# One pass over four row groups for the attention scores, with the values in the spare columns of the same banks

## The chip, the cores and the metric

The kernel runs on one core of one Trainium2 chip. The metric is the time of one execution on the device in microseconds (us), given as the median of several executions. Most executions of one kernel agree within 0.3%. For each one the mean granted clock of TensorE is known as well, as a share of full speed. One execution of each version was profiled. Below, a group of matmuls *holds the queue* from its first start to the first start of the group behind it.

## The reference

Windowed attention with eight batches, eight heads, 576 positions and 64 channels is followed by a feed-forward network (FFN) that multiplies two projections.

```python
scores = scale * np.matmul(q, k.transpose(0, 1, 3, 2))
rel = pos[:, None] - pos[None, :]
mask_plain = (rel >= 0) & (rel < 32)                         # heads 0 to 3
mask_dil = (rel >= 0) & (rel < 128) & (rel % 4 == 0)         # heads 4 to 7
attn = softmax(where(masks, scores, -1e9))                   # (shortened)
x = (attn @ v), heads side by side: 4608 tokens x 512
h = (x @ w1) * (x @ w2) @ w3                                 # 512 -> 1024 -> 1024
out = h @ w_out                                              # -> 4608 x 512, float32
```

The kernel multiplies `w3` and `w_out` into one matrix first. Below this is called fusing.

## The kernel before

The attention is cut into 32 steps: eight batches (called blocks here), two sets of four heads, two halves of the positions. Each step has four parts on TensorE: scores for heads 0 and 1, scores for heads 2 and 3, values (the product of exponentials and v), and transposes of the result. In between stand FFN matmuls of 128x512, so that the softmax on ScalarE and VectorE has time. `scores` of the kernel before, cut to what matters:

```python
ps_s = psum.tile([P, 2, TB], F32, name="ps_s")      # two banks for scores
ps_o = psum.tile([P, 2, TB], F32, name="ps_o")      # two banks for values
def scores(self, hp, sp):                           # hp: which pair of heads
    for m in range(3 * hf, 3 * hf + 3):
        for c in range(2):                          # two halves of the 64 channels
            for g in range(2):
                prt = slice(32 * (2 * hp + g), 32 * (2 * hp + g) + 32)
                nc.tensor.matmul(out=sp[:, g, c0 : c0 + 96], lhsT=kt[prt, ...], rhs=..., ...)
    nc.scalar.activation(out=ev, in_=sp[:, :, 0:HALF], func=ACT.Exp, scale=scale)  # 576 columns
    nc.vector.tensor_tensor(out=ev, in0=ev, in1=mk..., op=AL.mult)                 # mask
def values(self):                                   # twelve matmuls into ps_o, then
    nc.vector.reciprocal(out=rcp[0:96], in_=ov[:, :, :, D])
    nc.vector.tensor_tensor(out=xo[0:96], in0=ov[:, :, :, 0:D], in1=rcp..., op=AL.mult)
```

The parts are put into a list of phases, block by block. `segment(lo, hi)` pipelines the steps lo to hi-1. There are three segments: block 0, block 1, blocks 2 to 7. A function `point()` in the FFN code runs the next phases at given places. The transposes of q and k (on VectorE) were phases of their own.

The softmax here doesn't subtract the row's maximum and nothing guards it: scores larger than these inputs give would overflow.

## Time and profile before

The kernel before takes 289.62 us (median of 3 executions, 289.61 to 290.29).

| busy, us of a span of 288.0 | TensorE matmul | weight load | VectorE | ScalarE | GpSimd |
|---|---|---|---|---|---|
| before | 260.3 (90%) | 131.8 | 164.8 (57%) | 123.8 (43%) | 53.7 |

From 75 us on TensorE never stops, so its queue sets the end. What it doesn't show is the list of TensorE's waits. Each line gives what waited, what ended the wait, the sum in us, how often, and the longest:

```profile
PE ps_s L258 <- DVE kt L230: 10.1, 2, 9.1
PE ps_s L258 <- DVE kt L223: 2.7, 1, 2.7
PE ps_x L312 <- ACT w3T L461: 2.3, 2, 1.2
PE ps_x L312 <- DVE xo L297: 1.8, 2, 1.3
```

The first two are mostly the start, where the first q and k are loaded and transposed. The name to keep in mind is `xo`, the normalised result of a step: before, no scores (`ps_s`) ever waited for it.

### The profile page before, as it was taken

How to read it: one execution, taken by the hardware profiler on the slowest of the kernel's cores; microseconds unless marked ns; L12 is line 12 of the kernel's file. 1: busy time of each engine (PE TensorE's matmuls, PEld its weight loads, DVE VectorE, ACT ScalarE, POOL GpSimd, SP SyncE). 2: the span in 40 equal slices, each digit the busy share in tenths (PEclk: the TensorE clock that was granted, in tenths of full speed). 3: DMA queues.
4: the chain of work that ended last, by engine and by line, in shares of the span. 5: the costliest groups of instructions: out<-in, count | busy, mean ns of one | idle time of the engine just before them, and what ended most of it. 6: DMA issues, size and time to landing. Idle time of an engine off the chain costs nothing.

```text
span 288.0 us, 5662 instructions
## 1 busy us (share of the span) xinstructions
PE 260.3 (90%) x2336; PEld 131.8 (46%) x2336; DVE 164.8 (57%) x356; ACT 123.8 (43%) x200; POOL 53.7 (19%) x77
## 2 busy tenths in 40 slices
PE   0466988879899999999999999999999999999994
PEld 0353435444345545444444445445545544444441
DVE  5573385545798776767677767776764443222110
ACT  1543245543446455444544454455444433332422
POOL 8943512350042042006000600000000000000000
PEclk9999999999999999999999999999999999999999
DMA  7999999999069289567907991111111121111133
GB/s 102 156 207 190 198 211 210 202 194 144 0 102 171 75 166 173 80 116 130 137 36 124 145 147 42 39 36 39 39 36 39 36 56 55 36 73 36 48 85 126
DMA packets 50746, 30.51 MB, mean 106 GB/s; under 512 B 37920, under 2 KB 40992, under 8 KB 50720
## 3 DMA queue, kind: packets, MB, share of 16 engines
q0 software_dynamic: 45088, 20.71, 57.5%
q1 hardware_dynamic: 5632, 9.44, 10.9%
q8 instruction: 18, 0.29, 0.4%
q14 instruction: 8, 0.07, 0.1%
HBM read 41.41 MB, written 9.44 MB: 177 GB/s over the span
## 4 chain that ended last, share of the span: by engine, by line
PE 82%; DMA 9%; POOL 3%; ACT 2%; DVE 2%; issue 1%; POOLq 0%; ACTq 0%
PE f L406 41%; PE f L439 22%; PE ps_s L258 7%; DMA qn<-in_q_dram 5%; DMA w_sb<-in_moe_w_dram 4%; PE f L469 4%; PE ps_o L287 4%; PE ps_x L312 3%; PE ps_x L455 1%; ACT w3T L461 1%; POOL vst L137 1%; POOL vp L128 1%; POOL w_sb L155 1%; ACT et L268 0%; POOL qn L113 0%
## 5 line engine op out<-in xcount | busy, mean ns | idle before, releaser
L406 PE MATMUL f<-XT,w_sb 128*128 128x512 bf16 x576 | 138.8, 383 | 2.0 <-DMA w_sb<-in_moe_w_dram 1.3
L417 DVE TENSOR_TENSOR gt<-f,asb 128x512 bf16<-128x512 f32 x72 | 49.5, 687 | 55.5 <-PE f L406 55.3
L406 PEld LDWEIGHTS <-w_sb 128*128 128x128 bf16 x576 | 52.5, 98 | 61.1 <-issue 3.1
L439 PE MATMUL f<-wf_sb,gt 128*128 128x512 bf16 x288 | 70.8, 379 | 0.0
L416 ACT CAST asb<-f 128x512 bf16<-128x512 f32 x72 | 42.2, 586 | 54.3 <-PE f L406 49.6
L268 ACT ACTIVATE et<-ps_s 128x576 bf16<-128x576 f32 x60 | 39.2, 653 | 40.1 <-PE ps_s L258 39.9
L447 ACT COPY osb<-f 128x512 f32<-128x512 f32 x36 | 21.1, 586 | 45.7 <-PE f L439 45.7
L258 PE MATMUL ps_s<-qt,kt 32*128 32x96 bf16 x720 | 26.9, 206 | 13.8 <-DVE kt L230 10.1
L439 PEld LDWEIGHTS <-gt 128*128 128x128 bf16 x288 | 25.2, 98 | 25.2
L258 PEld LDWEIGHTS <-kt 32*128 32x128 bf16 x768 | 19.3, 97 | 37.0 <-issue 20.2
L297 DVE TENSOR_TENSOR xo<-ps_o,rcp 96x768 bf16<-96x768 f32 x32 | 30.5, 953 | 1.1
L137 POOL DMA_DIRECT2D vst<-in_v_dram x32 | 21.3, 672 | 13.9 <-DMA w3n<-in_moe_w_dram 4.4
L270 DVE TENSOR_TENSOR et<-et,mask_pl 128x576 bf16<-128x576 bf16 x32 | 14.6, 457 | 15.8 <-ACT et L268 15.5
L270 DVE TENSOR_TENSOR et<-et,mask_di 128x576 bf16<-128x576 bf16 x32 | 14.6, 456 | 14.7 <-ACT et L268 14.5
L230 DVE STREAM_TRANSPOSE qt<-qn 128x160 uint32<-128x160 uint32 (+1 forms) x64 | 19.6, 421 | 1.9 <-DMA qn<-in_q_dram 1.9
L287 PEld LDWEIGHTS <-et 128*128 128x128 bf16 x384 | 17.0, 102 | 7.7 <-issue 1.2
L312 PE MATMUL ps_x<-ident,xo 96*128 96x96 bf16 x192 | 14.4, 215 | 5.4 <-ACT w3T L461 2.3
L312 PEld LDWEIGHTS <-xo 96*128 96x128 bf16 x192 | 11.9, 102 | 12.5 <-DVE xo L297 4.1
L113 POOL DMA_DIRECT2D qn<-in_q_dram x9 | 6.3, 696 | 61.1 <-DVE qt L230 57.9
L296 DVE RECIPROCAL rcp<-ps_o 96x12 f32<-96x12 f32 x32 | 7.2, 225 | 16.4 <-PE ps_o L287 16.3
L469 PE MATMUL f<-wo_sb,w3T 128*128 128x512 bf16 x64 | 16.0, 380 | 0.0
L327 ACT COPY XT<-ps_x 128x576 bf16<-128x576 bf16 x18 | 11.5, 640 | 7.7 <-PE ps_x L312 7.7
(43 smaller groups left out, 113.8 us busy)
## 6 DMA issues: line engine op xcount, KB each, us to landing
qn<-in_q_dram POOLq DMA_DIRECT2D x7, 576.0 KB, 8.7
kn<-in_k_dram POOLq DMA_DIRECT2D x7, 576.0 KB, 7.8
vp<-in_v_dram POOLq DMA_DIRECT2D x7, 384.0 KB, 9.8
w_sb<-in_moe_w_dram POOLq DMA_DIRECT2D x4, 512.0 KB, 11.9
w3n<-in_moe_w_dram POOLq DMA_DIRECT2D x4, 512.0 KB, 18.7
out_dram<-osb SPq DMA_DIRECT2D x8, 256.0 KB, 2.3
out_dram<-osb SPq DMA_DIRECT2D x8, 224.0 KB, 2.3
out_dram<-osb SPq DMA_DIRECT2D x8, 192.0 KB, 2.2
```

The lines of the kernel that those rows point to most:

```text
L137: nc.gpsimd.dma_start(out=vsts[b % 2][p0 : p0 + n, m, :, :], in_=bass.AP(tensor=x.tensor, offset=x.offset + (4 * i0 + 2 * second) * D, ap= ...
L258: nc.tensor.matmul(out=sp[:, g, c0 : c0 + 96], lhsT=kt[prt, 96 * m : 96 * m + P, c], rhs=rhs, start=(c == 0), stop=(c == 1),)
L268: nc.scalar.activation(out=ev, in_=sp[:, :, 0:HALF], func=ACT.Exp, scale=scale)
L270: nc.vector.tensor_tensor(out=ev, in0=ev, in1=mk.unsqueeze(1).to_broadcast([P, 2, HALF]), op=AL.mult)
L287: nc.tensor.matmul(out=ps_o[:, hp, j * (D + 1) : (j + 1) * (D + 1)], lhsT=self.et[:, c0 : c0 + P], rhs=rhs, start=True, stop=True,)
L297: nc.vector.tensor_tensor(out=xo[0:96], in0=ov[:, :, :, 0:D], in1=rcp[0:96].unsqueeze(3).to_broadcast([96, 2, 6, D]), op=AL.mult,)
L312: nc.tensor.transpose(out=xo, in_=self.xo[0:96, hp, 2 * m : 2 * m + 2, :], identity=ident[0:96, 0:96],)
L406: nc.tensor.matmul(out=ps, lhsT=w_sb[:, c, f * P : (f + 1) * P], rhs=XT[:, c, t0 + lo : t0 + hi], start=(c == 0), stop=(c == DCH - 1),)
L416: nc.scalar.copy(out=a_sb[:, 0 : hi - lo], in_=ps)
L417: nc.vector.tensor_tensor(out=gts[t][:, f, lo:hi], in0=pss[1], in1=a_sb[:, 0 : hi - lo], op=AL.mult)
L439: nc.tensor.matmul(out=y, lhsT=gts[t][:, f, tb * P : (tb + 1) * P], rhs=wf_sb[:, f, :], start=(f == 0), stop=(f == KFF - 1),)
L469: nc.tensor.matmul(out=ps, lhsT=w3T[ft][:, g, :], rhs=wo_sb[:, g, :], start=(g == 0), stop=(g == KFF - 1),)
```

## The change

The intent is to compute the scores of all four heads in one pass. Head h lies on partitions 32h to 32h+31, which is called a row group here, so four heads fill four groups. The four results go to four banks (in this kernel slices of 512 float32 columns of the memory that takes TensorE's results). With the banks thus taken, the values go to the unused columns of the same banks (288 columns are scores, then 195 are values). The exponential and the mask become one instruction each, of 1152 columns. The core of the diff:

```diff
-    ps_s = psum.tile([P, 2, TB], F32, name="ps_s")
-    ps_o = psum.tile([P, 2, TB], F32, name="ps_o")
+    ps_a = psum.tile([P, 4, TB], F32, name="ps_a")
...
-        def scores(self, hp, sp):
+        def scores(self):
...
-                    for g in range(2):
-                        prt = slice(32 * (2 * hp + g), 32 * (2 * hp + g) + 32)
+                    for h in range(4):
+                        prt = slice(32 * h, 32 * h + 32)
...
+            n = 2 if self.b == 0 else 4
+            for h in range(0, 4, n):      # exponential and mask of n heads at once
...
+            if self.b == 0:
+                ov = ps_e[:, :, 0 : ns * (D + 1)]
+            else:
+                ov = ps_a[:, :, HALF : HALF + ns * (D + 1)]
...
-                later(lambda st=st: st.scores(0, s_tile(0)))
+                later(st.scores)
...
-                later(lambda st=st: st.scores(1, s_tile(1)))
                 if at == 0:
-                    later(transpose_qk, b, 0, 0)
+                    if i == lo:
+                        behind(transpose_qk, b, 0, 0)
...
```

`later` makes a phase of its own and `behind` hangs a function to the phase before it. Thus there are fewer phases, and they fall at other places between the FFN matmuls. From block 1 on the change also moves the transposes of q and k to earlier places; at the start of a segment two of them now fall behind the same scores.

More of the change, by code (lines that the diff above doesn't have):

```diff
@@ L258, in scores @@
                         nc.tensor.matmul(
-                            out=sp[:, g, c0 : c0 + 96],
+                            out=ps_a[:, h, c0 : c0 + 96],
                             lhsT=kt[prt, 96 * m : 96 * m + P, c],
@@ L264, in scores @@
                         )
-            ev = self.et[:, 2 * hp * HALF : 2 * (hp + 1) * HALF].rearrange(
-                "p (g x) -> p g x", g=2
-            )
-            nc.scalar.activation(out=ev, in_=sp[:, :, 0:HALF], func=ACT.Exp, scale=scale)
             mk = (mask_di if u else mask_pl[:, hf]).rearrange("p m x -> p (m x)")
-            nc.vector.tensor_tensor(
-                out=ev, in0=ev, in1=mk.unsqueeze(1).to_broadcast([P, 2, HALF]), op=AL.mult
-            )
+            n = 2 if self.b == 0 else 4
+            for h in range(0, 4, n):
+                ev = self.et[:, h * HALF : (h + n) * HALF].rearrange("p (g x) -> p g x", g=n)
+                nc.scalar.activation(
+                    out=ev, in_=ps_a[:, h : h + n, 0:HALF], func=ACT.Exp, scale=scale
+                )
+                nc.vector.tensor_tensor(
+                    out=ev, in0=ev, in1=mk.unsqueeze(1).to_broadcast([P, n, HALF]), op=AL.mult
+                )
         def values(self):
@@ L277, in values @@
             self.xo = xo = wk_pool.tile([P, 2, 6, D], BF16, tag="xo", bufs=3, name="xo")
+            nb = 2 if self.b == 0 else 4
+            ns = 12 // nb
+            if self.b == 0:
+                ov = ps_e[:, :, 0 : ns * (D + 1)]
+            else:
+                ov = ps_a[:, :, HALF : HALF + ns * (D + 1)]
+            ov = ov.rearrange("p n (j e) -> p n j e", e=D + 1)
             for hp in range(2):
@@ L280, in values @@
                     for hl in range(2):
-                        h, j = 2 * hp + hl, 2 * m + hl
+                        h, j = 2 * hp + hl, 6 * hp + 2 * m + hl
                         if self.u == 0:
@@ L287, in values @@
                         nc.tensor.matmul(
-                            out=ps_o[:, hp, j * (D + 1) : (j + 1) * (D + 1)],
+                            out=ov[:, j // ns, j % ns, :],
                             lhsT=self.et[:, c0 : c0 + P],
@@ L293, in values @@
                         )
-            rcp = wk_pool.tile([P, 2, 6], F32, tag="rcp", name="rcp")
-            ov = ps_o[0:96, :, 0 : 6 * (D + 1)].rearrange("p h (j e) -> p h j e", e=D + 1)
-            nc.vector.reciprocal(out=rcp[0:96], in_=ov[:, :, :, D])
+            rcp = wk_pool.tile([P, nb, ns], F32, tag=f"rcp{nb}", name="rcp")
+            nc.vector.reciprocal(out=rcp[0:96], in_=ov[0:96, :, :, D])
             nc.vector.tensor_tensor(
-                out=xo[0:96],
-                in0=ov[:, :, :, 0:D],
-                in1=rcp[0:96].unsqueeze(3).to_broadcast([96, 2, 6, D]),
+                out=xo[0:96].rearrange("p h j d -> p (h j) d").rearrange(
+                    "p (n s) d -> p n s d", n=nb
+                ),
+                in0=ov[0:96, :, :, 0:D],
+                in1=rcp[0:96].unsqueeze(3).to_broadcast([96, nb, ns, D]),
                 op=AL.mult,
@@ L327, in to_channels @@
                 nc.scalar.copy(out=dst, in_=xv)
-    early = [True]
     steps = [
@@ L346, in prefetch, with behind, run @@
             load_vp(b)
-    def s_tile(hp):
-        return ps_e if early[0] and hp else ps_s
     def later(f, *args):
-        phases.append(lambda: f(*args))
+        phases.append([lambda: f(*args)])
+    def behind(f, *args):
+        phases[-1].append(lambda: f(*args))
+    def run(phase):
+        for f in phase:
+            f()
     def segment(lo, hi):
@@ L366, in segment @@
                     later(spread_vd, b)
-            if at == 2 and more:
-                later(transpose_qk, b + 1, 1, 0)
-            if at == 3 and more:
-                later(transpose_qk, b + 1, 1, 1)
             if st is not None:
-                later(lambda st=st: st.scores(0, s_tile(0)))
+                later(st.scores)
             if p2 is not None:
@@ L378, in segment @@
             if st is not None:
-                later(lambda st=st: st.scores(1, s_tile(1)))
                 if at == 0:
-                    later(transpose_qk, b, 0, 0)
+                    if i == lo:
+                        behind(transpose_qk, b, 0, 0)
                     if b == 0:
-                        later(spread_vd, 0)
+                        behind(spread_vd, 0)
+                    else:
+                        behind(transpose_qk, b, 0, 1)
                 if at == 1:
-                    later(transpose_qk, b, 0, 1)
-                    later(prefetch, b + 2)
+                    if b == 0:
+                        behind(transpose_qk, b, 0, 1)
+                    behind(prefetch, b + 2)
+                    if more:
+                        behind(transpose_qk, b + 1, 1, 0)
+                if at == 2 and more:
+                    behind(transpose_qk, b + 1, 1, 1)
+                    behind(spread_vd, b + 1)
                 if at == 3 and more:
-                    later(spread_vd, b + 1)
+                    behind(transpose_qk, b + 1, 0, 0)
     segment(0, 4)
@@ L493 @@
     for ph in phases[:n0]:
-        ph()
-    early[0] = False
+        run(ph)
     stage.close()
@@ L511, in point @@
         while state[1] < want:
-            phases[state[1]]()
+            run(phases[state[1]])
             state[1] += 1
```

## The prediction

> **What bounds the kernel now.** I read the page's busy table and slices first, then the busy time by stage, then the order of instructions of one steady stretch in the timeline, then the waits that end TensorE's idle time.
>
> ```profile
> 37.30:75.10 37.80, 32.47 (x332) 17.75 (x332) 22.15 (x48) 16.53 (x22) 9.58 (x12) 1.00 1.25 176
> 75.10:102.70 27.60, 27.54 (x317) 14.21 (x318) 22.37 (x52) 14.26 (x24) 6.17 (x8) 1.00 0.75 101
> 102.70:230.50 127.80, 127.80 (x1234) 64.04 (x1233) 87.15 (x179) 61.85 (x104) 15.73 (x20) 1.00 0.54 86
> ```
>
> These are stages: first the stretch, its length, then busy us of TensorE matmul, weight load, VectorE, ScalarE, GpSimd. Before 37.3 us TensorE waits for data: two FFN weight halves land at 37.31 and end a wait of 1.32 us. From 37.3 to 75.1 block 1's attention runs beside the fusing of two weight matrices, with 5.3 us of TensorE idle. From 75 us to the end TensorE does not stop: every nanosecond of its queue is on the path that sets the end. ScalarE (61.85 of 127.80) and VectorE (87.15) have room. So what counts is the time the TensorE queue needs, and any new wait in it.
>
> The same queue at one steady place, by the starts of its groups:
>
> ```profile
> 153.88 0.62 PEld L287 LDWEIGHTS <-et 128*128 128x128 bf16 x12
> 154.09 0.53 PE L287 MATMUL ps_o<-vd,et 128*128 128x65 bf16 x12
> 154.37 0.69 DVE L417 TENSOR_TENSOR gt<-f,asb 128x512 bf16<-128x512 f32 x1 [0.80 <-PE f L406]
> ...
> 154.46 1.02 PE L439 MATMUL f<-wf_sb,gt 128*128 128x512 bf16 x4
> 154.97 0.22 DVE L296 RECIPROCAL rcp<-ps_o 96x12 f32<-96x12 f32 x1
> 155.23 0.95 DVE L297 TENSOR_TENSOR xo<-ps_o,rcp 96x768 bf16<-96x768 f32 x1
> 155.42 0.29 PEld L258 LDWEIGHTS <-kt 32*128 32x128 bf16 x12 [0.42 <-issue]
> 155.42 0.43 PE L258 MATMUL ps_s<-qt,kt 32*128 32x96 bf16 x12
> ...
> 155.78 0.55 PEld L439 LDWEIGHTS <-gt 128*128 128x128 bf16 x4
> 155.78 1.04 PE L439 MATMUL f<-wf_sb,gt 128*128 128x512 bf16 x4
> ```
>
> Four FFN matmuls take 0.86 us (0.216 each; eight elsewhere 1.73). Twelve value matmuls hold the queue 0.37 (154.09 to 154.46). But 154.46 to 155.42 is 0.96, so 0.10 is lost on entering the 32-row scores; the twelve score matmuls then hold it 0.36 to 155.78, and the first full matmul after them is some 0.01 late. One half of the scores (two heads) thus costs 0.47 us, two halves per step 0.94. A six-fold transpose group costs 0.26 (152.11 to 152.37). Sum per step: 0.94 + 0.37 + 0.26 = 1.57; with 24 FFN matmuls (5.18) that is 6.75, and the pattern does repeat after 26.99 us for four steps.
>
> Inside the 0.36 there are six rounds of two concurrent matmuls. The records last about 0.20, twelve span 0.43, so the last starts 0.23 after the first: some 43 ns per round, however many row groups are in it.
>
> **What the Trainium skill says.** "TensorEngine Tiling (Array Packing)", Key Properties: changing the tiling mode drains TensorE. The trace agrees: 0.10 lost going in, and a pause after the last 32-row matmul coming out (0.36 held, 0.23 of starts). "TensorE: Matmul & The Clock Gate", Part 3 (Measured speedup vs the span model): packed row tiles cost one matmul plus about 4 ns per further tile, with 3.07x measured for four row groups. The trace already has four groups running, at the cold clock, where the second pair of heads went to other banks:
>
> ```profile
> 18.64 0.27 PE L258 MATMUL ps_s<-qt,kt 32*128 32x96 bf16 x1
> 18.64 0.27 PE L258 MATMUL ps_e<-qt,kt 32*128 32x96 bf16 x1
> 18.64 0.27 PE L258 MATMUL ps_s<-qt,kt 32*128 32x96 bf16 x1
> 18.65 0.27 PE L258 MATMUL ps_e<-qt,kt 32*128 32x96 bf16 x1
> 18.72 0.27 PE L258 MATMUL ps_s<-qt,kt 32*128 32x96 bf16 x1
> ```
>
> Four start together, and the next round comes 80 ns later. "PSUM — Partial Sum Buffer", PSUM bank collisions: two engines may not use one bank and quadrant at once even at different columns, so guards go by bank. No trace shows a collision, but the built program obeys it: in the changed kernel scores wait for VectorE's normalisation (xo) of the previous values, and values wait for ScalarE's exponentials, although their columns are disjoint. Before, scores and values have banks of their own.
>
> **The change part by part.**
> *Score passes.* One pass of six rounds with four groups takes the place of two such passes. Cost by the above: 0.10 in, 0.36 plus some 0.02 for two more starts and the double number of instructions, 0.01 after: 0.49 or so against 0.94. Saved 0.45 us per step. This holds for the 28 steps beside FFN work; the four of block 0 lie before the 37.3 us arrival. Gross: 28 x 0.45 = 12.6 us.
>
> *Exponentials, mask.* ScalarE takes 653 ns for 576 columns and 586 and 1012 for copies of 512 and 1024: 0.83 ns a column, so my estimate for 1152 is 1.13 us in place of 1.31. The mask, 457 twice, becomes an estimated 0.76. Neither engine is the bound; worth nothing directly. But scores now read out as one 1.13 us piece instead of 0.65.
>
> *Steady order (blocks 3 to 7).* The built order is: scores, 8 FFN, transposes, 8 FFN, values, 8 FFN, scores. New wait: values, then reciprocal and xo, then scores. In the fence above: values start 154.09, gt 154.37, reciprocal 154.97, xo 155.23 to 156.18, plus 0.05 to be seen by TensorE (an xo that ends at 69.32 releases transposes at 69.38): 2.14 after the values' start. TensorE gets to the scores after 0.37 + 1.73 + 0.10 = 2.20. It just fits, with 0.06 us to spare. VectorE is free for that gt: transposes 1.2, spread 0.55, mask 0.76 and first gt, copy are over about 0.9 earlier. Values find exponentials done since 2 us. So 18 steps (14 to 31) gain nearly all: 18 x 0.45 = 8.1, less an allowance of 0.03 each for the thin margin: 7.5.
>
> *Fusing stage (steps 4 to 7).* Walking the built order with these durations, TensorE waits 0.4 at step 5 (for the exponential of step 4: only four FFN matmuls lie between), three times 1.26 for the fused weight's copy in the shared bank (before: 1.22, 1.28, 1.28), 0.5 each at steps 6 and 7 for xo (again only four FFN matmuls after values), 0.4 and 0.6 at transposes. Sum 6.1, against 5.3 idle to 75.1 before. But the 1.00 wait there for the transposed k of block 2 goes: four more fusing matmuls and four more of FFN now stand behind it. Passes save 4 x 0.45 = 1.8. Net of all, about 2 us ahead at step 8.
>
> *Block 2 and the start of block 3 (steps 8 to 13).* Here the phases lie densely. Values of 8 wait 0.4 for exponentials of 9. Then the worst: both of the next half's transposes (1.23 + 1.25) now queue ahead of two gt, a mask and xo on VectorE; I get xo of step 8 ended 7.8 us after step 8's scores, TensorE there at 5.2: a wait of 2.6. Steps 11, 12, 13 have four FFN matmuls between values and scores: 2.14 + gt delays against 1.33, 0.5 to 0.6 each. Sum 4.8. Passes save 6 x 0.45 = 2.7. Net loss 2.1.
>
> *Sum:* 2 - 2.1 + 7.5 = 7.4 us. 289.6 - 7.4 = 282.2, call it 282.
>
> *Start.* Block 0 now computes both exponentials before the next scores; I expect its end some 0.8 us later, inside the 1.32 of waiting for weights. Nothing.
>
> **The rivals.**
> (a) *The new wait eats the gain.* In steady steps, anything that delays gt by over 0.06 makes VectorE's chain set the step. If it costs 0.2 per step, 3.6 us go: 285.5. For it: the thin margin, and VectorE at 68% (87.15 of 127.80). Against: VectorE loses an instruction per step and its work ahead of gt has slack.
> (b) *Four groups do not run at 43 ns a round.* Weight loads and matmuls are 8 instructions per round, 5.4 ns each; the cold rounds of 80 ns do not test that. At 65 ns a round each step loses 0.13: 28 x 0.13 = 3.6 us, again near 285.5. If they ran one pair after the other, only the switch of some 0.2 would be saved: 28 x 0.2 = 5.6, less the 6 of new waits: no gain.
> (c) *The waits of block 2 are shorter than in my walk,* because the scheduler's buffers let FFN work pass, or VectorE overlaps. Without the 4.8 it would be 277.5.
> (d) *Hidden anyway.* Against it: TensorE is busy 127.80 of 127.80.
>
> **Range and chances.** Centre 282. Rival (c) in part gives 279.5; (a) or (b) nearly in full 285.5. The 2% line is 283.8, which needs about 1.8 us more loss than I count: I give faster 0.76, within 2% 0.23, slower 0.01.
>
> **What would show it.** Score groups of 24 that hold the queue 0.37 to 0.40; a steady repeat of about 25.2 us per four steps instead of 26.99; exponentials of 1152 columns near 1.13 us; in the list of waits, scores (ps_a) released by xo with one of over 2 us near step 10 and some of half a microsecond, and almost none after block 3. Wrong if steady scores wait for xo in most steps, if the score group holds over 0.5, or if FFN starts late enough to move the 37.31.

## The result

The changed kernel takes 283.26 us (median of 4 executions, 282.31 to 283.40), the kernel before in the same rounds 289.63 us (289.61 to 290.29). The ratio is 0.9768 with a 95% interval of 0.9742 to 0.9793: faster by 2.3%. Ratios are the mean time of one kernel's executions over that of the other's of the same rounds, so they are not quite the ratio of the medians. The forecast was 282.0 with a range of 279.5 to 285.5.

The stages of the changed kernel, in the same form as the prediction's first fence (stretch, its length, busy us of TensorE matmul, weight load, VectorE, ScalarE, GpSimd; then the granted clock):

```profile
36.86:74.16 37.30, 31.13 (x330) 17.21 (x337) 22.47 (x46) 16.15 (x20) 9.57 (x12) 1.00 1.28 180
74.16:104.63 30.47, 25.19 (x307) 13.08 (x312) 23.89 (x49) 13.52 (x18) 9.67 (x14) 0.94 0.77 102
104.63:217.00 112.37, 111.32 (x1158) 56.84 (x1176) 78.24 (x151) 54.79 (x82) 12.20 (x15) 1.00 0.58 92
```

The second stretch is step 8 to step 14, that is block 2 and the start of block 3. By its records TensorE is idle for 5.3 of these 30.47 us (five matmuls have no record), where it was busy without a stop before, and the clock is 0.94. In the third stretch it is busy again but for about 1 us, of which at least a part is matmuls whose record is missing (1158 matmuls have 1176 weight loads).

A steady stretch, in the order of time (start, length, engine, line, operation), to be held against the second fence of the prediction:

```profile
108.74 0.53 PE L297 MATMUL ps_a<-vd,et 128*128 128x65 bf16 x12
109.01 0.69 DVE L436 TENSOR_TENSOR gt<-f,asb 128x512 bf16<-128x512 f32 x1 [1.21 <-PE f L425]
109.11 1.89 PE L458 MATMUL f<-wf_sb,gt 128*128 128x512 bf16 x8
109.61 0.22 DVE L305 RECIPROCAL rcp<-ps_a 96x12 f32<-96x12 f32 x1
109.87 0.95 DVE L306 TENSOR_TENSOR xo<-ps_a,rcp 96x768 bf16<-96x768 f32 x1
...
110.92 0.44 PE L258 MATMUL ps_a<-qt,kt 32*128 32x96 bf16 x24
...
111.30 0.39 PE L425 MATMUL f<-XT,w_sb 128*128 128x512 bf16 x1
```

All 24 score matmuls hold the queue from 110.92 to 111.30, some 0.37 us, as twelve did before. `xo` ends at 109.87 + 0.95 = 110.82, and the scores that need its bank start 0.10 later with no wait put down. Four steps now take 25.15 us (104.64 to 129.78), against 26.99.

The waits of TensorE after:

```profile
PE ps_a L258 <- DVE kt L229: 7.9, 1, 7.9
PE ps_a L258 <- DVE xo L306: 5.1, 6, 2.2
PE ps_x L323 <- DVE xo L306: 4.0, 4, 1.3
...
PE ps_x L323 <- ACT w3T L480: 2.6, 3, 1.2
```

The second line is new: scores wait for `xo` six times, 5.1 us in all, once 2.2. That one is before step 10. And the softmax instructions (count, then busy us and mean ns of one):

```profile
L269 ACT ACTIVATE et<-ps_a 128x1152 bf16<-128x1152 f32 (+1 forms) x36 | 36.5, 1026 | 18.3 <-PE ps_a L258 18.3
...
L272 DVE TENSOR_TENSOR et<-et,mask_pl 128x1152 bf16<-128x1152 bf16 (+1 forms) x18 | 12.4, 692 | 14.3 <-ACT et L269 14.2
```

These means mix in block 0's pieces of 576. A single exponential of 1152 columns takes 1.13 to 1.14 us in the timeline, a mask 0.73 to 0.76.

One thing nobody had asked about shows in the table of two-microsecond windows around step 10 (same columns as above):

```profile
78.00:80.00 2.00, 1.39 (x16) 0.74 (x16) 2.00 (x4) 0.53 (x2) 1.60 (x3) 1.00 0.31 18
80.00:82.00 2.00, 0.24 (x23) 0.24 (x23) 1.97 (x5) 0.15 (x1) 2.00 (x4) 1.00 0.99 180
82.00:84.00 2.00, 1.67 (x24) 0.76 (x12) 1.37 (x5) 1.13 (x1) 1.86 (x2) 0.50 1.10 206
84.00:86.00 2.00, 2.00 (x13) 0.86 (x12) 0.83 (x2) 0.23 (x1) 0.00 (x0) 0.64 1.11 195
```

After the wait, TensorE runs at half its clock from about 82.0 to 85.4 us (a mean of 0.64 over two microseconds is 1.44 us at half). From the scores of step 10 to the transposes behind the next eight FFN matmuls it takes 3.75 us (81.76 to 85.51) where it takes 2.12 in the steady stretch (110.92 to 113.04). These eight have eight weight loads but only seven records: the first one's is missing, so the 0.33 us of idle time that the timeline shows behind the scores is no wait. In the kernel before, the clock is 1.00 in these windows.

### The profile page after: what moved, and what is told of

Read it like the earlier page. It is cut to its first block, busy times and chain, and to the rows that moved or that the text cites. A ratio compares the mean times of both kernels' runs of the same rounds, so it can differ in the third digit from the quotient of the medians.

```text
span 281.5 us, 5593 instructions
## 1 busy us (share of the span) xinstructions
PE 245.9 (87%) x2300; PEld 125.7 (45%) x2336; DVE 160.1 (57%) x328; ACT 117.8 (42%) x172; POOL 53.6 (19%) x77
## 4 chain that ended last, share of the span: by engine, by line
PE 75%; DMA 9%; DVE 6%; POOL 3%; ACT 3%; issue 2%; POOLq 0%; ACTq 0%; DVEq 0%
PE f L425 39%; PE f L458 22%; DMA qn<-in_q_dram 5%; DMA w_sb<-in_moe_w_dram 4%; PE ps_a L258 4%; PE f L488 4%; PE ps_a L297 3%; PE ps_x L323 3%; DVE xo L306 2%; ACT w3T L480 1%; PE ps_x L474 1%; POOL vst L136 1%; DVE gt L436 1%; DVE qt L229 1%; ACT et L269 1%
## 5 line engine op out<-in xcount | busy, mean ns | idle before, releaser
L425 PE MATMUL f<-XT,w_sb 128*128 128x512 bf16 x550 | 136.5, 387 | 3.4 <-issue 0.9
L458 PE MATMUL f<-wf_sb,gt 128*128 128x512 bf16 x282 | 67.2, 379 | 0.4 <-issue 0.2
L269 ACT ACTIVATE et<-ps_a 128x1152 bf16<-128x1152 f32 (+1 forms) x36 | 36.5, 1026 | 18.3 <-PE ps_a L258 18.3
L458 PEld LDWEIGHTS <-gt 128*128 128x128 bf16 x288 | 26.5, 98 | 28.5
L258 PE MATMUL ps_a<-qt,kt 32*128 32x96 bf16 x768 | 15.1, 211 | 18.5 <-DVE kt L229 7.9
L306 DVE TENSOR_TENSOR xo<-ps_a,rcp 96x768 bf16<-96x768 f32 x28 | 26.7, 953 | 1.0
L258 PEld LDWEIGHTS <-kt 32*128 32x128 bf16 x768 | 10.9, 97 | 30.5 <-issue 16.9
L272 DVE TENSOR_TENSOR et<-et,mask_pl 128x1152 bf16<-128x1152 bf16 (+1 forms) x18 | 12.4, 692 | 14.3 <-ACT et L269 14.2
L272 DVE TENSOR_TENSOR et<-et,mask_di 128x1152 bf16<-128x1152 bf16 (+1 forms) x18 | 12.3, 687 | 9.8 <-ACT et L269 9.7
L480 ACT COPY w3T<-ps_x 128x1024 bf16<-128x1024 bf16 x8 | 8.1, 1012 | 8.4 <-PE ps_x L474 8.4
```

The costliest lines, as they stand in the source:

```text
L258: nc.tensor.matmul(out=ps_a[:, h, c0 : c0 + 96], lhsT=kt[prt, 96 * m : 96 * m + P, c], rhs=rhs, start=(c == 0), stop=(c == 1),)
L269: nc.scalar.activation(out=ev, in_=ps_a[:, h : h + n, 0:HALF], func=ACT.Exp, scale=scale)
L272: nc.vector.tensor_tensor(out=ev, in0=ev, in1=mk.unsqueeze(1).to_broadcast([P, n, HALF]), op=AL.mult)
L306: nc.vector.tensor_tensor(out=xo[0:96].rearrange("p h j d -> p (h j) d").rearrange("p (n s) d -> p n s d", n=nb), in0=ov[0:96, :, :, 0:D], ...
L425: nc.tensor.matmul(out=ps, lhsT=w_sb[:, c, f * P : (f + 1) * P], rhs=XT[:, c, t0 + lo : t0 + hi], start=(c == 0), stop=(c == DCH - 1),)
L458: nc.tensor.matmul(out=y, lhsT=gts[t][:, f, tb * P : (tb + 1) * P], rhs=wf_sb[:, f, :], start=(f == 0), stop=(f == KFF - 1),)
```

## The experiments

My theory after the result: the gain is the score pass, 0.46 us per step, as predicted; the loss is in block 2, as predicted, but larger, because the 2.2 us wait also costs clock. The rivals: the lighter ScalarE and VectorE are the gain; the regrouping of the phases is; the thin margin before the scores is not what it looks like; the clock falls for another reason. All results below are correct against the reference. Runs 1, 2, 4 and 5 shared one chip (kernel before 289.99), 3, 6, 7 and 8 another set of rounds (289.60), 9 and 10 a third (289.79).

### 1. Two passes again, everything else changed

```diff
-                later(st.scores)
+                later(st.scores, (0,))        # heads 0 and 1
+                later(st.scores, (1,))        # heads 2 and 3, then exponential and mask
...
-                later(p2.to_channels)
+                (behind if st is not None else later)(p2.to_channels)
```

> Undoes the merged pass alone: the changed kernel, but each step's scores are two passes of 12 matmuls on two row groups with FFN matmuls between them; exponential, mask, banks and the values' columns stay as changed. Theory (the gain is one 32-row pass fewer per step, 0.46 us each): steady repeat of four steps back from 25.14 to about 27.0 us, 28 steps x 0.46 = 12.9 us, so about 296 us, 2% slower than the kernel before, because the new waits for shared banks stay. Rival (the gain comes from the fewer and longer instructions on ScalarE and VectorE and the steadier spacing of phases): within 2 us of the changed kernel, 283 to 285.

Measured: 294.32 us (293.96 to 295.08), ratio to before 1.0155, interval 1.0134 to 1.0176, clock 0.998 to 1.000. From its timeline:

```profile
107.39 0.43 PE L258 MATMUL ps_a<-qt,kt 32*128 32x96 bf16 x12
107.76 1.90 PE L428 MATMUL f<-XT,w_sb 128*128 128x512 bf16 x8
109.59 0.44 PE L258 MATMUL ps_a<-qt,kt 32*128 32x96 bf16 x12
109.96 0.43 PE L325 MATMUL ps_x<-ident,xo 96*128 96x96 bf16 x6
```

Twelve matmuls hold the queue 0.37 us (107.39 to 107.76; 109.59 to 109.96), as long as 24 in the changed kernel. Four steps take 27.00 us (107.39 to 134.39), just what they took before the change. So the one pass is the whole gain of the steady blocks. The rest of the change alone is a loss: 294.32 against 289.99 is 4.3 us. The expected 296 was missed by 1.7 us; that the clock doesn't fall here, as it does in the changed kernel, would account for it.

### 2. One pass, but pair after pair

```diff
-            for m in range(3 * hf, 3 * hf + 3):
+            for hp, m in [(hp, m) for hp in range(2) for m in range(3 * hf, 3 * hf + 3)]:
                 for c in range(2):
-                    for h in range(4):
+                    for h in (2 * hp, 2 * hp + 1):
```

> One pass, one switch, but the 24 matmuls are issued head pair after head pair (12 on row groups 0 and 1, then 12 on 2 and 3) instead of round by round over all four. Theory: part of the 0.46 is concurrency of four groups, part the saved switch of some 0.2. In the kernel before, at the cold clock, a second pair issued like this began 0.156 us after the first and then ran beside it, so I expect the score group to hold the queue 0.37 + about 0.15 = 0.52 us: 28 x 0.15 = 4 us slower than the changed kernel, some 287. Rival 1 (the four groups never overlap, only the switch was saved): no change, 283.3. Rival 2 (issued like this nothing overlaps): 0.37 + 0.24, 290. Rival 3 (TensorE reorders freely over its queue): no change in time, but then the group holds the queue 0.37 and records of all four groups start together.

Measured: 285.14 us (284.13 to 286.35), ratio 0.9837, interval 0.9801 to 0.9872. The direction was right and the size too large. The pass holds the queue 0.48 us, a steady step takes 6.39 instead of 6.285 us. The starts of the single matmuls in one pass, from the trace:

```
118.676 118.679 118.732 118.735 118.776 118.779 118.788 118.791 118.819 118.824 118.843 118.848 ...
```

They read as two series with steps of some 44 ns: one from 118.676, one from 118.788. So the second pair, though issued behind all twelve matmuls of the first, starts 0.112 us after it and then runs beside it. (The records name no row group, so that reading rests on the spacing.) Of the 0.46 us per step, 0.105 needs the interleaved order, and the other 0.36 needs only that nothing stands between the two pairs. The medians mix executions with and without the fall of the clock: one of four here (0.994, 286.35 us), three of four in the changed kernel. The profiled executions, both with it, differ by 3.15 us (286.35 against 283.20), and 28 x 0.105 is 2.9.

### 3. Exponentials and masks in two pieces

```diff
-            n = 2 if self.b == 0 else 4
+            n = 2
```

> The changed kernel with the exponential and the mask of every step again in two pieces of 576 columns instead of one of 1152. My theory (TensorE's instruction time in the score passes is what was gained; ScalarE and VectorE beside it were not what bound the kernel): ScalarE and VectorE do about 0.2 us more each per step, but nothing on TensorE waits for it in the steady blocks; 283.2 to 283.9 us, and the steady four steps stay at 25.15 us. Rival (the fewer, larger exponentials and masks are the gain, about 0.2 us for each of 28 steps on VectorE): at least 286, and the four steps at 25.9 or more.

Measured: 283.38 us (283.20 to 283.63), ratio 0.978, interval 0.9765 to 0.9794; three steps take 18.86 us (110.86 to 129.72), so four 25.14. The exponentials are 64 of 654 ns again. Nothing changes: the softmax instructions were not what was gained. The wait before step 10 is 2.01 us here, and the clock is 0.991 to 0.993 in all four executions.

### 4. Block 2's transposes ahead of step 8

The wait before step 10 is one for `xo` of step 8, and on VectorE two transposes of q and k stand ahead of it. Here both go to the end of the stage before, where VectorE has room.

```diff
+                if i == 9 and st is None:
+                    behind(transpose_qk, 2, 0, 1)
             if p1 is not None:
                 later(p1.values)
+                if i == 8 and st is None:
+                    behind(transpose_qk, 2, 0, 0)
...
-                    if i == lo:
+                    if i == lo and b < 2:
...
-                    else:
+                    elif not (i == lo and b == 2):
```

> The changed kernel; only the two groups of VectorE transposes for heads 0 to 3 of block 2 are moved from behind step 8's scores into the end of the fusing stage, where VectorE waits for TensorE. Theory (the 2.23 us wait before step 10's scores is VectorE's backlog of 2.46 us of transposes ahead of xo, and that wait lets the TensorE clock fall to half for some 3.6 us): the wait shrinks to about 1.1 us, the granted clock stays 1.00, 1.1 + 1.6 us saved, about 280.6. Rival (clock dip is chance, or another wait of the same size takes its place, such as the mask of step 9): 282.2 to 283.3, and the clock still dips.

Measured: 280.72 us (280.51 to 281.07), ratio 0.9684, interval 0.9668 to 0.97, clock 0.997 to 1.000. The longest wait of scores for `xo` is now 1.1 us (scores still wait 4.0 us in all, in six waits), and the clock stays at 1.00 in all windows from 78 to 88 us. Step 8 to step 14 takes 27.74 us instead of 30.48. This was as expected, and it is already better than both kernels.

### 5. One segment for blocks 1 to 7

A new segment starts with phases that lie densely, and block 2's loss comes of that. So why not one segment?

```diff
-    segment(4, 8)
-    segment(8, 4 * B)
+    segment(4, 4 * B)
```

> The changed kernel with blocks 1 to 7 in one run of phases: block 2's transposes and its first steps are prepared while block 1 still runs, so the steps are not drained between blocks 1 and 2, and eight FFN matmuls stand between values and scores almost everywhere. Theory (what is lost against 28 x 0.46 = 12.9 us is the dense start of block 2, 4 to 5 us of waits for xo and exponentials plus 1.6 us at half clock): most of that returns, 278 to 280. Rival (the losses are in the fusing stage's waits for the shared transpose bank, which stay): 281.5 to 283.

Measured: 284.67 us (283.73 to 285.50), ratio 0.9828, interval 0.9805 to 0.9852, clock 0.986 to 0.988. The expectation was missed by 5 us. Two lines of its timeline tell why (in brackets the idle time before, and what ended it):

```profile
54.72 1.20 DVE L229 STREAM_TRANSPOSE qt<-qn 128x160 uint32<-128x160 uint32 x4 [8.03 <-DMA qn<-in_q_dram]
...
58.89 0.35 PE L258 MATMUL ps_a<-qt,kt 32*128 32x96 bf16 x8 [5.99 <-DVE xo L306]
```

In the merged order VectorE comes to block 2's transposes before the load of block 2's q has landed. It stands for 8.03 us, everything behind it is late, `xo` too, and TensorE stands for 5.99 us. The clock then falls to half here as well (0.50 in 56 to 62 us). I had looked at the phases and not at when the data land.

### 6. A longer chain before the scores

```diff
+            if self.b >= 3:
+                nc.vector.memset(idle, 0.0)          # 128 x 256 float32
             nc.vector.reciprocal(out=rcp[0:96], in_=ov[0:96, :, :, D])
```

> The changed kernel with one memset of 128 x 256 float32 on VectorE ahead of each reciprocal from block 3 on (some 0.27 us by the memsets of the first 20 us). My theory (in the steady blocks the chain values, reciprocal, xo, scores has just 0.05 us to spare against the eight matmuls between them): about 0.2 us of each memset shows as a wait before the scores, 24 steps in all of which some 18 to 22 lie beside the FFN: 287 to 288.5 us, the steady four steps at 25.9 to 26.1. Rival (the order in the queue leaves more room than the profile makes it look, VectorE's work is hidden): 283.2 to 284.

Measured: 285.45 us (284.45 to 286.72), ratio 0.9853, interval 0.982 to 0.9885.

```profile
115.24 0.27 DVE L307 MEMSET idle<- 128x256 f32 x1
115.43 0.17 DVE L308 RECIPROCAL rcp<-ps_a 96x12 f32<-96x12 f32 x1
115.63 0.95 DVE L309 TENSOR_TENSOR xo<-ps_a,rcp 96x768 bf16<-96x768 f32 x1
...
116.64 0.44 PE L259 MATMUL ps_a<-qt,kt 32*128 32x96 bf16 x24
```

A steady step takes 6.46 us instead of 6.285, so 0.17 of the memset's 0.27 shows. The reciprocal is 0.05 shorter behind it (0.17 instead of 0.22), so the spare time before the scores is about 0.05, as read from the changed kernel's timeline. The mechanism held; the total fell short of the expected 287. I had counted 24 memsets where there are 20, and in the profiled execution the clock did not fall after the wait before step 10, although that wait was 2.2 us here too. Its four executions had clocks of 0.998, 0.993, 0.992 and 0.998 with 285.05, 285.84, 286.72 and 284.45 us: the two with the lower clock are 1.5 us longer in the mean. So the fall of the clock happens in some executions and not in others; why is taken up below.

### 7. Transposes as phases of their own again

```diff
-                        behind(transpose_qk, b, 0, 0)
+                        later(transpose_qk, b, 0, 0)
...                                                     # likewise all others, the spreading and the prefetch
```

> The changed kernel with the transposes of q and k, the spreading of v and the prefetch in phases of their own again, as in the kernel before, so that values and the next scores stand further apart in places (16 matmuls of the FFN rather than 8) and step 10 has 8 matmuls between values of step 8 and its own scores. My theory (one score pass is the gain, the hanging of VectorE work behind a phase is not needed for it): steady four steps 25.1 to 25.3 us; block 2 loses less to waits than in the changed kernel, so 281 to 284 us. Rival (the regrouping of phases is what made the gain possible): 286 or more.

Measured: 281.94 us (281.35 to 283.01), ratio 0.9734, interval 0.9708 to 0.9759. Its four steps from step 15 take 25.14 us (111.06 to 136.20). The regrouping was not needed for the gain; undone, the kernel is 1.3 us faster. Scores wait for `xo` only 0.8 us in all, and the profiled execution keeps a clock of 0.998. Most of the 1.3 us may be the clock: three executions here (0.997 to 1.000) take 281.35 to 282.27 us, and the changed kernel's one without the fall takes 282.31. The fourth here had 0.992 and 283.01 us, and no trace.

### 8. One segment, block 2's transposes later

```diff
-    segment(4, 8)
-    segment(8, 4 * B)
+    segment(4, 4 * B)
...
+                late = b == 1 and more       # block 2's transposes: behind values of steps 6 and 7,
...                                          # once its q and k have landed
```

> One segment for blocks 1 to 7, as in the run that missed its expectation, but with block 2's transposes put behind values of steps 6 and 7, after block 2's q and k have landed (data at about 54.7 us in that run). My theory of that miss (an 8 us wait of VectorE for the load of block 2, which held xo and so TensorE for 6.0 us and left the clock at half): without it no wait on TensorE of over 1.5 us in 50 to 90 us, clock 1.00 there, and 277.5 to 280.5 us. Rival (one segment is bad for another reason, such as VectorE's transposes holding up the copies of the fused weight): 283 or more with waits before the fusing matmuls.

Measured: 278.96 us (278.30 to 279.99), ratio 0.9637, interval 0.9608 to 0.9667. The expectation held in time and clock (1.00 in all windows from 50 to 104 us). One part of it didn't: a wait of 2.4 us for the transposed k remains in the fusing stage. (One of the four executions, not the profiled one, had a clock of 0.994 and 279.55 us.) So the miss of run 5 was the load, not the merging of segments.

### 9. The changed kernel with its wait filled

```diff
+    def fill():                              # nine 128x512 matmuls, result unread
+        ps = bank()
+        for n in range(9):
+            nc.tensor.matmul(out=ps, lhsT=w1_sb[:, 0, 0:P], rhs=XT[:, 0, 0:TB], ...)
...
+                if i == 10:
+                    later(fill)
+                    behind(st.scores)
```

> The changed kernel with nine 128x512 matmuls whose result nobody reads (about 1.9 us at 0.215 us each) put directly ahead of the scores of step 10, where TensorE otherwise stands still for 2.2 us waiting for xo. They lie within the wait, so they take no time themselves. My theory (the standstill is what lets the granted clock fall to half for some 3 us afterwards, and that costs about 1.6 us): clock 1.00 in 82 to 86 us, the scores of step 10 hold the queue for 0.37 us and the eight matmuls after them for 1.74 us again, and 281.4 to 282.4 us. Rival (the clock falls there for another reason, such as the dense score pass drawing on a power limit, or its fall costs nothing because something else is waited for afterwards): half clock as before, or full clock at 283.0 to 283.8 us.

Measured: 282.10 us (281.63 to 282.48, 5 executions), ratio 0.9736, interval 0.9716 to 0.9757, clock 0.998 to 1.000 in all five.

```profile
80.00:82.00 2.00, 1.95 (x9) 0.75 (x9) 1.97 (x4) 0.59 (x1) 2.00 (x4) 1.00 0.91 135
82.00:84.00 2.00, 1.74 (x32) 0.97 (x32) 1.44 (x6) 1.13 (x1) 2.00 (x3) 1.00 1.11 203
84.00:86.00 2.00, 2.00 (x26) 1.28 (x25) 1.51 (x3) 1.13 (x2) 0.42 (x1) 1.00 1.13 211
```

TensorE is busy with useless work in the wait (1.95 of 2.00, where it was 0.24), step 10 still waits for the same `xo`, and the clock stays at 1.00. From step 8 to step 14 it takes 28.83 us (74.71 to 103.54) instead of 30.48: 1.65 less, for more work. The standstill is what lets the clock fall.

### 10. The two best edits together

Run 8 with run 7's edit: all transposes, the spreading and the prefetch in phases of their own.

> The two best edits together: one segment with block 2's transposes placed late (278.96 us in its run) and the transposes in phases of their own (281.94 alone, 1.4 below the changed kernel). If the second edit was worth 1.4 us only because it shortened the wait before step 10 and with it kept the clock up, there is nothing left of that to gain here: 278.5 to 280 us. If the spacing of phases is worth something in itself: 277 to 278.

Measured: 276.28 us (275.87 to 276.62), ratio 0.9536, interval 0.9515 to 0.9556. This is the best version: 13.5 us below the kernel before, where the change alone gives 6.4. It went past what either reading expected. From 36.8 us to 90 us the waits listed for TensorE add up to 6.0 us against 7.2 in run 8. The 2.4 us for the transposed k there are 1.0 in two waits here:

```profile
PE ps_a L258 <- DVE kt L229: 1.0, 2, 0.8
PE ps_a L258 <- DVE xo L306: 0.4, 1, 0.4
```

So the spacing of the phases is worth something by itself, beside the clock: both profiled executions run at a clock of 1.00 from some 31 us until the last 1.2 us of the span.

## Why the prediction was right, and where it was off

It was right: 283.26 in a range of 279.5 to 285.5, and faster by over 2% as its likeliest case. To compare its three stages with the measured ones, I take the moment at which step 8's and step 14's scores start, and count the FFN matmuls done by then from the weight loads, of which no record is missing. A difference in that count is worth 0.216 us each.

| | before: us, FFN done | after: us, FFN done | after is ahead by | gained in the stage | predicted |
|---|---|---|---|---|---|
| step 8 | 75.12, 72 | 74.16, 76 | 0.96 + 4 x 0.216 = 1.82 | +1.8 | +2 |
| step 14 | 105.35, 172 | 104.63, 160 | 0.72 - 12 x 0.216 = -1.87 | -3.7 | -2.1 |
| end of span | 288.0 | 281.5 | 6.5 | +8.4 | +7.5 |

**Score passes.** The estimate was 0.49 us for the one pass and 0.45 saved per step. Measured: 0.10 on entering and 0.37 of holding, 0.46 saved. Run 1 shows that this alone is the steady gain. Rival (b), slower rounds with four groups, is out: the starts come in fours, within some 10 ns, every 43 ns (in the steady pass at 148.635 us).

**Exponentials, mask.** Estimated 1.13 and 0.76 us, measured 1.13 to 1.14 and 0.73 to 0.76; "worth nothing directly" is what run 3 shows.

**Steady order.** The spare of 0.06 us was right (0.05 by run 6). Rival (a), that the new wait eats the gain, did not come: the allowance of 0.03 per step was not needed and a pass saved 0.465 instead of 0.45, which makes this stage 8.4 (18 x 0.465) instead of 7.5.

**Fusing stage.** "About 2 us ahead at step 8" became 1.8. Of this, 0.45 is luck that I had not counted: in the profiled execution the second halves of the FFN weights start to be used at 36.86 instead of 37.31. And the prediction's own terms don't add up to 2. The 1.00 us wait that goes is part of the 5.3 us of idle time before, so it was counted twice: 5.3 - 6.1 + 1.8 is 1.0. Without the early start the stage gained 1.4. The predicted waits for the fused weight's copy (three of 1.26) are there as 2.6 + 1.1 us.

**Block 2 and the start of block 3.** The mechanism was right: the longest wait is the one before step 10, for `xo` behind two transposes, 2.23 us instead of 2.6. Scores of step 10 start 7.60 us after step 8's, predicted 7.8. Run 4 takes the transposes away, and the wait falls to 1.1. The sum of the waits was right too. These are the waits of the changed kernel from step 8 to step 14 alone, 4.6 us where the walk had 4.8:

```profile
PE ps_a L258 <- DVE xo L306: 4.2, 4, 2.2
...
PE ps_a L297 <- ACT et L269: 0.4, 1, 0.4
```

Yet the term "net loss 2.1" was too small by 1.6, and this is the miss of the sum; the 0.9 that the steady stage gave on top hid more than half of it. I treated a wait as costing its own length. The 2.23 us of standstill also took half the clock for the 3.4 us after it, and run 9, which fills the standstill and changes nothing else, gets 1.65 us of it back.

The Trainium skill has this mechanism. "TensorE: Matmul & The Clock Gate", Part 1 (What's actually happening), says that idle time drops the TensorE clock to half, judged over a free-running window of about 3.4 us. The prediction cites another part of that page and does not apply this one; its longest wait was shorter than that window. Traces agree on the half, on the 3.4 us for which it lasts, and on the window as well, which shows for the traced executions why the clock falls in one and not in another.

In all twelve traces the records of the clock, which begin with its first rise at some 30 us, change at whole multiples of 3.413 us after that rise. (That the clock was low at 18.64 us, as the prediction says, is read from its rounds of 80 ns against 43.) In the changed kernel it rises at 30.81 us, falls 15 windows later at 82.01 and rises one window later at 85.42. The whole standstill of 2.23 us lay in the window that ended at 82.01. In run 6 a wait of 2.21 us (80.25 to 82.46) was cut by the boundary at 80.68 of that trace's own grid. The windows are, first the changed kernel's and then run 6's:

```profile
78.60:82.01 3.41, 1.18 (x31) 0.54 (x27) 3.38 (x8) 0.59 (x1) 3.02 (x6) 1.00 0.76 117
77.27:80.68 3.41, 2.61 (x44) 1.26 (x33) 3.41 (x9) 1.93 (x3) 1.58 (x3) 1.00 0.27 24
80.68:84.10 3.42, 1.64 (x30) 0.89 (x30) 2.86 (x8) 1.32 (x2) 3.42 (x5) 1.00 1.00 185
```

TensorE was busy 1.18 us in the first, and half clock followed; 2.61 and 1.64 in the others, and it did not. Over all traces, counted from the first rise, every window with 1.39 us or less of busy time was followed by half clock (runs 2, 3 and 5 have 1.17, 1.39, 0.80 and 0.03, besides the windows at the kernels' ends), and none with 1.50 or more. So the length of a standstill does not decide alone; where it lies against the windows does too, and that differs from execution to execution. Three of the changed kernel's four executions have a clock of 0.991 to 0.993 (283.20 to 283.40 us) and the fourth 0.997 (282.31 us). Only the first of these was traced, so for the others, and for the single lower clocks in runs 7 and 8, this is the likely reason and not a shown one.

How far this accounting carries can be seen in all the versions. Each is set against the changed kernel at the start of step 14, where 160 FFN matmuls were done, or more. The lead there is the lead at the end of the span:

| version | step 14: us, FFN done | lead at step 14 | span, lead at the end |
|---|---|---|---|
| changed kernel | 104.63, 160 | | 281.5 |
| 4, transposes earlier | 102.50, 160 | 2.13 | 279.4, 2.1 |
| 5, one segment | 105.13, 160 | -0.50 | 282.0, -0.5 |
| 7, own phases | 104.77, 168 | 8 x 0.216 - 0.14 = 1.59 | 279.9, 1.6 |
| 8, late block 2 | 99.76, 160 | 4.87 | 276.6, 4.9 |
| 9, wait filled | 103.54, 160 | 1.09 | 280.4, 1.1 |
| 10, both | 99.75, 168 | 4.88 + 8 x 0.216 = 6.61 | 274.9, 6.6 |

After step 14 all of them run the same. Everything that these edits won or lost lies before step 14, in the waits and in what they do to the clock. (Run 9 starts step 8 some 0.55 us later than the changed kernel, which is why its lead is 1.09 and not 1.65.)

What stays open: which part of the 2.7 us between the medians of runs 8 and 10 is their waits. The profiled executions differ by 1.7 us. The listed waits explain 1.5 of it: unrounded they are 7.2 us in run 8 and 5.7 in run 10, where two of "issue", 0.3 together, are places of missing matmul records and left out. Run 8's executions spread over 1.7 us.

## What to carry to other kernels

Where one engine is busy without a stop, count what its queue is held by, not the busy time of its records: 24 matmuls in four row groups hold it as long as 12 in two. Buffers that are merged for it bring new waits; walk the order at the places where the pipeline starts anew, since the steady state hides nothing there, and check when loads land before moving work up. A standstill of TensorE of some two microseconds may cost most of its own length a second time through the clock (here 1.65 us for 2.23), in some executions and not in others, so fill or shorten the longest one first, and compare executions of like clock.

## What the Trainium skill lacked or had wrong

- "TensorE: Matmul & The Clock Gate", Why this matters for your kernels, warns of idle gaps over about 3 us. Here a wait of 2.23 us was followed by 3.4 us at half clock in the profiled execution. The page doesn't say how idle a window must be: here those with TensorE busy 1.39 of 3.41 us or less were followed by half clock, and those with 1.50 or more were not. What helps and is not said there: nine unread matmuls in the gap kept the clock at 0.998 to 1.000 in five of five executions.
- The same page, Part 3 (The mechanism), says that matmuls start and end strictly in program order. In run 2, matmuls of the second pair start at 118.788 us, between those of the first (118.776 and 118.819), although all of the first pair's are issued ahead. This is read from the spacing of the starts.
- "TensorEngine Tiling (Array Packing)", Key Properties, names the drain on changing the mode without a size. Here entering the 32-row scores from full matmuls costs 0.10 us, in every step.
- No page says what sharing a bank costs in time. "PSUM — Partial Sum Buffer", PSUM bank collisions, gives the rule that the built kernel follows. Here it made scores wait for `xo` six times, 5.1 us in all, at the places where only four FFN matmuls, or two transposes on VectorE, stood in between.
